# The planner of a fused HGRN2 attention and FFN kernel: DMA transfers planned as a queue, later loads for chunks 5 to 7

## The chip, the cores and the metric

The kernel runs on one core of one Trainium2 chip. The time of a run is the device time of that core in microseconds, and the time of a kernel is the median of its runs. The engines are named as in the profile: PE is the tensor engine's matmul, PEld its weight load, DVE the vector engine, ACT the scalar engine, POOL the general-purpose engine, SP the engine that issues nearly all DMA transfers here. Each engine executes its own instructions in the order in which they were written.

## The reference

Two stages follow each other. The first is a gated linear attention, the second a feed-forward network with a product in the place of an activation function.

```python
f = 1.0 / (1.0 + np.exp(-f_logit))            # B, H, S, D = 4, 8, 768, 48
for t in range(S):
    state = f[:, :, t, :, None] * state + np.einsum('bhd,bhe->bhde', k[:, :, t], v[:, :, t])
    y[:, :, t] = np.einsum('bhd,bhde->bhe', q[:, :, t], state)
x = y.transpose(0, 2, 1, 3).reshape(B * S, H * D)   # 3072 tokens x 384
out = (((x @ w1) * (x @ w2)) @ w3) @ w_out         # 384 -> 1024 -> 1024 -> 384
```

The inputs of the attention are float32. The four weights are float64, and the kernel reads their 64-bit words as pairs of 32-bit words.

## The kernel before, in words

**Tiling.** The 4 x 768 tokens are cut into 24 chunks of 128 tokens, called units u, six for each of the four sequences. The feed-forward network works on six blocks of 512 tokens, that is, four chunks each. A tile of q, k or f of one chunk has 112 partitions (two groups of 48 with a gap) and 512 columns.

**The attention of a chunk.** `front(u)` loads f, k and q (two DMA transfers of 96 KB each, L366 to L368) and v (one of 192 KB). ACT takes the sigmoid (`gates`, L380). DVE scans the products of the gates forward (L388) and backward (L410) and scales q (L404) and k (L418) with them. PE forms the pairs q times k (L431), transposes K (L455), and multiplies with v and with the state that is carried on. ACT copies the results out of PSUM: A (L562), kt (L589), the blocks of the state for the first chunks (`blocks`, L699), the last gate products (L393) and the outcome ys (L710). DVE updates the state (L689, L690). POOL masks A (L571). The first four chunks use one form of these steps and turn ys into xt on PE and ACT (`moved` L739, `settled` L744). The later chunks use half-size products, and write ys to DRAM (`written`, L731, two transfers) and read it back transposed as xt (`gathered`, L734, one transfer).

**The weights.** `fetch` (from L1103 on) loads a piece of a weight (L1138) into one of the landing places of the tile `place` and converts its words: ACT takes the magnitude (L1157) and the other word (L1160), DVE shifts (L1163, L1164), sets the sign (L1168) and joins (L1174). A landing place is free for a later piece once the pieces that used it before have passed DVE. There are twelve pieces of w1 and w2 (512 KB each), four of w_out (768 KB) and eight of w3 (1 MB). PE multiplies w3 with w_out once (`fold`, L1221), so that each token needs only the product with the folded matrix wc.

**The feed-forward network.** Block 0 forms `a` and `b` with plain products on PE (`part`; its products are issued by L761, as most products of this stage are), ACT keeps `a` (`keep_a`, L798) and DVE multiplies `b` into it (L803). Block 1 does this for half of its columns, for chunks 4 and 5 first and then for 6 and 7; the rest of block 1 and the later blocks use a scheme of seven products instead of eight (`seven`), with sums of xt made by DVE (L831). `down` multiplies with wc in the same way, and two stores (L1053) write each part of the output.

**What sets the order.** Nothing above is written in its final order. The class `Plan` gathers tasks, each with an engine, a cost in microseconds, its dependencies, a priority, and a `lag` that a task on another engine has to wait for after it. `order` is a list scheduler: again and again it takes, of all tasks whose dependencies are planned, the one that can start first (then by priority, then by number), and puts it at that time. At the end the tasks are emitted in the order of the planned starts, and this fixes the order of each engine's instructions. The planned times do not reach the chip: there an instruction waits for what it needs, and what stands behind it on its engine waits too. Before the first planned PE task, and where the plan has PE idle in the first 35 us (`FULL`), warm-up products (L268) are put in.

A transfer is planned by `moves` as a task of SP (0.45 us, the issue) and a task of an engine called DMA (bytes over a rate). At most eight transfers are under way, by the slot `lane`: an issue waits for the one eight places before it to have landed.

The lines that the change touches are those of `Plan.add`, `Plan.order`, `moves`, the loads and the costs in `front`, the calls of `moves` for yt and xt in `rest`, and the one for a weight piece in `fetch`.

Of the kernel before, what the change touches and what calls it, by code (L numbers as in the profile page):

```python
# [52 lines left out]
KM = DM // P  # L53
# [14 lines left out]
HIGH = float.fromhex("0x1.dffffep+16")  # L68
W = C // 2
FULL = 35.0  # L70
FLOOR = 2.0**-60
RANGE = 2.0**-40


class Plan:
# [13 lines left out]

        self.pools[name] = [None] * n  # L90

    def add(self, eng, cost, emit, deps=(), prio=0.0, takes=(), frees=(), lag=0.2, slack=0.0):


        t = {
            "eng": eng, "cost": cost, "emit": emit, "deps": [d for d in deps if d is not None], "prio": prio,
            "takes": list(takes), "frees": list(frees), "lag": lag, "slack": slack, "at": None, "end": None, "no": len(self.tasks),
        }
        self.tasks.append(t)
        return t  # L100

    def order(self):
        free, done, left = {}, [], list(self.tasks)
        enders = {}
        for t in self.tasks:
            for f in t["frees"]:
                enders.setdefault(id(f), []).append(t)

        def after(t, ds):

            if any(d["end"] is None for d in ds):
                return None
            return max([0.0] + [d["end"] + (d["lag"] + t["slack"] if d["eng"] != t["eng"] else 0.0) for d in ds])

        def places(t, name):

            ends = [(after(t, enders[id(h)]) if h else 0.0, i) for i, h in enumerate(self.pools[name])]
            return [e for e in ends if e[0] is not None]

        def start(t):  # L120

            waits, at = list(t["deps"]), free.get(t["eng"], 0.0)
            for name in t["takes"]:
                if name in self.pools:
                    ends = places(t, name)
                    if not ends:
                        return None
                    at = max(at, min(ends)[0])
                    continue
                n, taken = self.slots[name]  # L130
                if len(taken) >= n:
                    waits += enders[id(taken[-n])]
            ready = after(t, waits)
            return None if ready is None else max(at, ready)

        while left:
            at, _, _, t = min(
                ((at, t["prio"], t["no"], t) for t in left if (at := start(t)) is not None), key=lambda x: x[:3]
            )
            t["at"], t["end"] = at, at + t["cost"]  # L140
            free[t["eng"]] = t["end"]
            for name in t["takes"]:
                if name in self.pools:
                    t["got"] = min(places(t, name))[1]
                    self.pools[name][t["got"]] = t
                else:
                    self.slots[name][1].append(t)
            left.remove(t)
            done.append(t)
        return sorted(done, key=lambda t: (t["at"], t["no"]))  # L150
# [44 lines left out]
def ranged(ctx, tc, q, k, f_logit, v, w1, w2, w3, w_out, out, ident, w12, wc, left):  # L195
# [56 lines left out]
    plan = Plan()  # L252
# [73 lines left out]
    def past(u, n, *names):  # L326
        return [tk[u - n][nm] for nm in names if u >= n and nm in tk[u - n]]

    def moves(n, size, rate, emit, deps, prio, late=0.0):


        for j in range(n):
            i = plan.add("SP", 0.45, (lambda: None) if j else emit, [d] if j else deps, prio - j * 1e-3, takes=["lane"], lag=0.6)
            d = i
            t = plan.add("DMA", size / n / rate, lambda: None, [i], prio - j * 1e-3, lag=1.3 + late, frees=[i])
        return t

    def loaded(dst, u):
# [3 lines left out]
    def front(u):  # L342

        s, t = st[u], tk[u]
        n0 = need(u)

        def load(dst, src):
            def emit():
                if dst is fs[0] and u == 0:

                    nc.sync.dma_start(dst[0:64], src[u].rearrange("two d n -> (two d) n")[0:64])
                    nc.sync.dma_start(dst[rows(1)], src[u, 1])
                    return
                for par in range(2):
                    nc.sync.dma_start(dst[rows(par)], src[u, par])
            return emit

        fu, qu, ku = (x[u if u < 4 else u % n] for x, n in ((fs, 2), (qs, 3), (ks, 2)))

        def free(n, *names):  # L360

            if u < 4:
                return []
            return asked[8:9] + [tk[u - n if u - n >= 4 else u % n][nm] for nm in names]

        t["lf"] = moves(2, 197, 250, load(fu, f_logit), free(2, "g"), n0 - 30)  # L366
        t["lk"] = moves(2, 197, 250, load(ku, k), free(2, "k"), n0 - 29.5)
        t["lq"] = moves(2, 197, 250, load(qu, q), free(3, "q"), n0 - 29)  # L368

        def load_v():  # L370
            s["v"] = at(12288 + NQ, DM) if u == 3 else loads.tile([P, DM], F32, name="vt")
            loaded(s["v"], u)

        t["lv"] = moves(
            1, 197, 320, load_v, [] if u == 3 else past(u, 4 if u in (4, 5, 6) else 3, "v", "s"),
            n0 - (28.2, 28.2, 28.2, 29.6, 12)[min(u, NPE)],
        )

        def gates():
            nc.scalar.activation(gate[u % 2][:, 0:NQ], fu, AF.Sigmoid)  # L380

        t["g"] = plan.add("ACT", 0.65, gates, [t["lf"]] + past(u, 2, "r") + past(u, 3, "G"), n0)
        if u % NCH and "G" in tk[u - 1]:
            tk[u - 1]["G"]["deps"].append(t["g"])

        def forward():
            s["P"] = one.tile([R, NQ], F32, name="fwd")
            nc.vector.tensor_tensor_scan(s["P"], gate[u % 2][:, 0:NQ], floor, 0.0, ALU.mult, ALU.max)  # L388

        t["p"] = plan.add("DVE", 1.25, forward, [t["g"]] + past(u, 1, "q", "i", "l"), n0)  # L390

        def last():
            nc.scalar.copy(lasts[:, u], heads(s["P"])[:, :, C - 1])  # L393

        t["l"] = plan.add("ACT", 0.2, last, [t["p"]], n0)

        def ends():
            nc.vector.reciprocal(heads(back)[:, :, C - 1], heads(s["P"])[:, :, C - 1])

        t["i"] = plan.add("DVE", 0.18, ends, [t["p"]] + past(u, 1, "r"), n0)  # L400

        def scale_q():
            s["Q"] = work3.tile([R, NQ], F32, name="Q")
            nc.vector.tensor_tensor(s["Q"], qu, s["P"], ALU.mult)  # L404

        t["q"] = plan.add("DVE", 0.7, scale_q, [t["p"], t["lq"]] + past(u, 3, "v", "a"), n0 + 0.1)

        def backward():
            s["R"] = one.tile([R, NQ], F32, name="bwd")
            nc.vector.tensor_tensor_scan(  # L410
                s["R"][:, ::-1], gate[u % 2][:, NQ:0:-1], back[:, ::-1], 0.0, ALU.mult, ALU.max
            )

        t["r"] = plan.add("DVE", 1.25, backward, [t["i"]] + past(u, 1, "k"), n0)

        def scale_k():
            s["K"] = work.tile([R, NQ], F32, name="K")
            nc.vector.tensor_tensor(s["K"], ku, s["R"], ALU.mult)  # L418

        t["k"] = plan.add("DVE", 0.7, scale_k, [t["r"], t["lk"]] + past(u, 2, "a", "t"), n0)  # L420
        if u in (2, 3):
            t["k"]["frees"].append(coming)

# [206 lines left out]
    def rest(u):  # L630
        s, t = st[u], tk[u]
        opens, closes = u % NCH == 0, u % NCH == NCH - 1
        n0 = need(u)
        if u < NPE:
# [6 lines left out]
                takes=["f"],  # L641
# [76 lines left out]
        n = u // UB  # L718
# [27 lines left out]
        before = blk[n - 2]["up"] if n >= 2 else []  # L746
        if u < NPE:
            t["z"] = plan.add("PE", 1.6, moved, [t["y"]], n0 - 996, takes=["f"], frees=[moving])
            t["x"] = plan.add("ACT", 0.55, settled, [t["z"]] + before, n0 - 20, frees=[t["z"]])
        else:  # L750
            t["z"] = moves(2, 197, 250, written, [t["y"]], n0 - 100)
            t["x"] = moves(1, 197, 250, gathered, [t["z"]] + before, n0 - 100)


    blk = [{} for _ in range(NB)]
# [353 lines left out]
    def fetch(loads_, a, prio, subs, deps=()):  # L1109
# [5 lines left out]
        total = subs[-1][1]  # L1115
        if not wide:
# [7 lines left out]
            waits = [d for sub in subs for d in sub[4]]  # L1124
            ld = plan.add("SP", 1.9 * total / 512, plain, waits, prio, lag=2.0)
            return [ld] * len(subs)
        load_no = len(users)
# [6 lines left out]
        held = holders(where, 2 * total)  # L1134

        def load():
            for place_, src in loads_:
                nc.sync.dma_start(raw.rearrange("p (a m) -> p a m", a=a)[place_], src.bitcast(U32))  # L1138

        ld = moves(1, total, 380, load, held, prio, max(0.0, 3.5 - 1.2 * load_no) if load_no < 4 * KM else 3.0)  # L1140
        asked.append(ld)
        got = []
        users.append((where, 2 * total, got))
# [179 lines left out]
    for t in plan.order():  # L1323
        if t["eng"] == "PE" and t["at"] < FULL:
            n = int((t["at"] - ready_at) / 0.43)
# [343 lines left out]
```

## Time and profile before

| | us |
|---|---|
| median of 3 runs | 477.67 (477.29 to 477.99) |
| profiled execution, its own time | 482.72 |
| profiled execution, span of the core | 481.0 |
| PE busy | 468.7 |
| PEld busy | 400.4 |
| DVE busy | 362.8 |
| ACT busy | 141.1 |
| POOL busy | 62.5 |

The mean granted clock of PE is 0.995 of full speed. The profiled execution took 5.05 us more than the median of the runs. Busy times of different engines overlap; the largest of them does not say alone what a change in one stage is worth. An instruction's line of the profile gives its start, its length, what it writes and reads, and in brackets how long its engine had been idle and what ended that. A transfer goes from its issue on SP to its landing.

### The profile page before, as it was taken

To read this page: it belongs to the slowest core of one execution; us is meant where nothing else is said; L and a number is where in the kernel's file an instruction comes from. 1 tells how busy PE (TensorE), PEld (TensorE's weight loads), DVE (VectorE), ACT (ScalarE), POOL (GpSimd) and SP (SyncE) were. 2 spreads that over 40 slices of the span, in tenths; PEclk is the share of its full clock that TensorE was granted. 3 is DMA by queue.
4 is the path that set the end of the run, shared out by engine and by line. 5 is a ranking of instruction groups with operands and counts; after the bars stand their busy time and mean duration, and the time that the engine had idled before them with its cause. 6 is when DMAs were issued, how large, how long until landed. Compare 5 with 4: busy or idle time off the path is not lost.

```text
span 481.0 us, 11341 instructions
## 1 busy us (share of the span) xinstructions
PE 468.7 (97%) x4667; PEld 400.4 (83%) x4667; DVE 362.8 (75%) x706; ACT 141.1 (29%) x310; POOL 62.5 (13%) x88
## 2 busy tenths in 40 slices
PE   8899999999999899999999999999999999999996
PEld 7788644656799688889988889988899888889995
DVE  7999699999999689899999567357653667664541
ACT  4697456462313334432432110001100110110000
POOL 9300000013303133312422100000000000000000
PEclk9999999999999899999999999999999999999999
DMA  6899277743415566446531002000111000000011
GB/s 183 269 387 236 54 278 246 260 138 100 134 50 162 163 172 169 115 132 169 148 110 46 18 18 65 34 33 2 34 33 58 9 0 1 0 1 1 34 66 37
DMA packets 36618, 50.10 MB, mean 104 GB/s; under 512 B 4546, under 2 KB 26050, under 8 KB 35538
## 3 DMA queue, kind: packets, MB, share of 16 engines
q1 hardware_dynamic: 36562, 49.33, 33.6%
q8 instruction: 37, 0.61, 0.6%
q14 instruction: 19, 0.16, 0.1%
HBM read 40.67 MB, written 8.65 MB: 103 GB/s over the span
## 4 chain that ended last, share of the span: by engine, by line
PE 73%; DVE 13%; DMA 6%; POOL 3%; issue 2%; ACT 1%; SPq 1%; DVEq 0%; POOLq 0%; ACTq 0%
PE f L761 62%; DVE place L1168 2%; PE f L1221 2%; DMA place<-in_w_dram 2%; PE py L515 2%; DVE place L1174 2%; DMA place<-in_w_out_dram 2%; PE f L455 2%; PE pa L441 2%; PE pa L548 2%; PE py L534 1%; DMA f<-in_f_logit_dram 1%; SPq L1138 1%; POOL ab L306 1%; DVE place L1253 1%
## 5 line engine op out<-in xcount | busy, mean ns | idle before, releaser
L761 PE MATMUL f<-xt,w 128*128 128x256 f32 (+1 forms) x600 | 162.8, 401 | 3.2 <-ACT gate L380 2.0
L761 PEld LDWEIGHTS f<-xt,w 128*128 128x128 f32 x600 | 114.1, 192 | 29.5 <-issue 10.0
L761 PE MATMUL f<-place 128*128 128x192 f32 (+1 forms) x504 | 112.1, 349 | 0.1
L761 PEld LDWEIGHTS f<-place 128*128 128x128 f32 x504 | 87.7, 190 | 6.2 <-DVE place L1010 0.4
L571 POOL TENSOR_SCALAR_AFFINE_SELECT A<-A 64x512 f32<-64x512 f32 (+1 forms) x44 | 40.7, 925 | 120.3 <-ACT A L565 110.5
L1221 PE MATMUL f<-place 128*128 128x384 f32 x128 | 42.8, 489 | 0.2 <-DVE place L1174 0.2
L864 ACT COPY a<-f 128x256 f32<-128x256 f32 x36 | 13.4, 373 | 93.2 <-PE f L761 78.0
L1221 PEld LDWEIGHTS f<-place 128*128 128x128 f32 x128 | 23.8, 190 | 16.5 <-DVE place L1174 0.8
L761 PE MATMUL f<-xt,place 128*128 128x256 f32 x144 | 37.3, 382 | 0.0
L761 PE MATMUL f<-wc,ab 128*128 128x192 f32 x192 | 35.2, 327 | 0.0
L761 PEld LDWEIGHTS f<-wc,ab 128*128 128x128 f32 x192 | 32.0, 190 | 0.5
L410 DVE TENSOR_TENSOR_SCAN bwd<-gate,back 112x512 f32<-112x512 f32 x24 | 30.0, 1249 | 0.8
L388 DVE TENSOR_TENSOR_SCAN fwd<-gate,floor 112x512 f32<-112x512 f32 x24 | 29.6, 1233 | 1.1 <-ACT gate L380 0.3
L761 PEld LDWEIGHTS f<-xt,place 128*128 128x128 f32 x144 | 26.6, 189 | 3.3
L888 DVE TENSOR_TENSOR place<-f,a 128x256 f32<-128x256 f32 x36 | 15.3, 424 | 18.6 <-PE f L761 18.4
L1157 ACT ACTIVATE place<-place 128x512 f32<-128x512 f32 (+2 forms) x24 | 21.3, 886 | 8.2 <-DVE w L1174 3.8
L1160 ACT ACTIVATE place<-place 128x512 f32<-128x512 uint32 (+2 forms) x24 | 21.1, 885 | 5.1 <-DMA place<-in_w_out_dram 5.1
L674 POOL TENSOR_TENSOR G<-lasts,gate 112x4 f32<-112x4 f32 x20 | 11.1, 556 | 87.3 <-ACT lasts L393 55.2
L710 ACT ACTIVATE ys<-py 112x512 f32<-112x512 f32 x20 | 11.9, 596 | 35.6 <-PE py L534 34.6
L761 PE MATMUL f<-place,w 128*128 128x256 f32 x72 | 21.4, 379 | 0.0
L899 DVE TENSOR_TENSOR ab<-f,place 128x256 f32<-128x256 f32 x36 | 15.2, 423 | 6.2 <-PE f L761 5.3
L997 DVE TENSOR_TENSOR place<-ab 128x512 f32<-128x512 f32 x24 | 16.9, 702 | 3.5 <-PE f L761 3.5
(126 smaller groups left out, 642.9 us busy)
## 6 DMA issues: line engine op xcount, KB each, us to landing
place<-in_w_dram SPq DMA_DIRECT2D x8, 1024.0 KB, 4.7
place<-in_w_dram SPq DMA_DIRECT2D x12, 512.0 KB, 9.7
out_dram<-o SPq DMA_DIRECT2D x24, 192.0 KB, 1.9
q<-in_q_dram SPq DMA_DIRECT2D x46, 96.0 KB, 2.8
vt<-in_v_dram SPq DMA_DIRECT2D x23, 192.0 KB, 3.4
k<-in_k_dram SPq DMA_DIRECT2D x44, 96.0 KB, 2.3
f<-in_f_logit_dram SPq DMA_DIRECT2D x43, 96.0 KB, 2.5
yt<-ys SPq DMA_DIRECT2D x40, 96.0 KB, 2.4
```

The lines of the kernel that those rows point to most:

```text
L388: nc.vector.tensor_tensor_scan(s["P"], gate[u % 2][:, 0:NQ], floor, 0.0, ALU.mult, ALU.max)
L410: nc.vector.tensor_tensor_scan(s["R"][:, ::-1], gate[u % 2][:, NQ:0:-1], back[:, ::-1], 0.0, ALU.mult, ALU.max)
L571: nc.gpsimd.affine_select(out=a, in_=a, pattern=pattern, compare_op=ALU.is_ge, fill=0.0, base=0, channel_multiplier=-1,)
L710: nc.scalar.activation(ys, py, AF.Copy, accum_out=ysum[:, u : u + 1])
L761: nc.tensor.matmul(out_, lhsT=lhs[i], rhs=rhs[i], start=start and i == 0, stop=i == len(lhs) - 1, skip_group_check=True,)
L864: nc.scalar.copy(q["a"], q["X"])
L888: nc.vector.tensor_tensor(ups["u3", k], q["Y"], q["a"], ALU.add)
L899: nc.vector.tensor_tensor(m if which else to(tok, half), q[bank_], m, ALU.add)
L997: nc.vector.tensor_tensor(abs_[j], x, y, op)
L1157: nc.scalar.activation(m, hi.bitcast(F32), AF.Abs)
L1160: nc.scalar.activation(lo.bitcast(F32), lo, AF.Copy, bias=2.0, scale=2.0**-51)
L1221: nc.tensor.matmul(w3s["p", jc], lhsT=w3s[jc][:, kc * P : kc * P + P], rhs=wos[:, kc], start=(kc == 0), stop=(kc == KF - 1),)
```

## The change

The planner's picture of the DMA transfers and of the early part is changed; no instruction of the computation is added or taken away.

- Every engine's planned time begins at 0.6 (`BEGIN`) instead of 0.
- Of several DMA tasks that could start first, the one asked for first is taken (`rank`), where before the priority decided.
- In two windows of planned time (`CROWDED`) a transfer's cost is multiplied by 1.6 or 1.3.
- Rates for f, k, q and yt go from 250 to 300, for weights from 380 to 400. The lag after an issue goes from 0.6 to 0.85, after a transfer from 1.3 to 1.1. The extra lag of a weight piece, which was 3.5 falling by 1.2 for each of the first pieces, then 0, and 3.0 for those of w_out and w3, becomes 0.5 for all.
- `scale_k` is planned at 1.3 for chunks 1 to 3, and at 0.72 for others, instead of 0.7; `scale_q` at 0.72.
- A task may have a time `since` before which it isn't planned. f, k and q of chunks 5 to 7 get one: 22 us (`AHEAD`) before the time at which the chunk is due.

```diff
+BEGIN = 0.6
+SURE = 0.5
+SURE_X = 0.0
+SURE_W = 2.0
+CROWDED = [(13.5, 19.5, 1.6), (33.0, 46.0, 1.3)]
+AHEAD = 22.0
...
     def order(self):
-        free, done, left = {}, [], list(self.tasks)
+        free, done, left = dict.fromkeys(("PE", "DVE", "ACT", "POOL", "SP"), BEGIN), [], list(self.tasks)
...
-            waits, at = list(t["deps"]), free.get(t["eng"], 0.0)
+            waits, at = list(t["deps"]), max(free.get(t["eng"], 0.0), t["since"])
...
+        def rank(t):
+            return t["deps"][0]["end"] - 1e6 if t["eng"] == "DMA" else t["prio"]
+        def slower(t, at):
+            return max([1.0] + [by for a, b, by in CROWDED if a <= at < b]) if t["eng"] == "DMA" else 1.0
...
-                ((at, t["prio"], t["no"], t) for t in left if (at := start(t)) is not None), key=lambda x: x[:3]
+                ((at, rank(t), t["no"], t) for t in left if (at := start(t)) is not None), key=lambda x: x[:3]
             )
-            t["at"], t["end"] = at, at + t["cost"]
+            t["at"], t["end"] = at, at + t["cost"] * slower(t, at)
...
-    def moves(n, size, rate, emit, deps, prio, late=0.0):
+    def moves(n, size, rate, emit, deps, prio, late=0.0, since=0.0):
...
-            i = plan.add("SP", 0.45, (lambda: None) if j else emit, [d] if j else deps, prio - j * 1e-3, takes=["lane"], lag=0.6)
+            i = plan.add("SP", 0.45, (lambda: None) if j else emit, [d] if j else deps, prio - j * 1e-3, takes=["lane"], lag=0.85, since=since)
             d = i
-            t = plan.add("DMA", size / n / rate, lambda: None, [i], prio - j * 1e-3, lag=1.3 + late, frees=[i])
+            t = plan.add("DMA", size / n / rate, lambda: None, [i], prio - j * 1e-3, lag=1.1 + late, frees=[i])
...
-        t["lf"] = moves(2, 197, 250, load(fu, f_logit), free(2, "g"), n0 - 30)
-        t["lk"] = moves(2, 197, 250, load(ku, k), free(2, "k"), n0 - 29.5)
-        t["lq"] = moves(2, 197, 250, load(qu, q), free(3, "q"), n0 - 29)
+        since = n0 - AHEAD if 4 < u < 8 else 0.0
+        t["lf"] = moves(2, 197, 300, load(fu, f_logit), free(2, "g"), n0 - 30, since=since)
+        t["lk"] = moves(2, 197, 300, load(ku, k), free(2, "k"), n0 - 29.5, since=since)
+        t["lq"] = moves(2, 197, 300, load(qu, q), free(3, "q"), n0 - 29, since=since)
...
-        t["q"] = plan.add("DVE", 0.7, scale_q, [t["p"], t["lq"]] + past(u, 3, "v", "a"), n0 + 0.1)
+        t["q"] = plan.add("DVE", 0.72, scale_q, [t["p"], t["lq"]] + past(u, 3, "v", "a"), n0 + 0.1)
...
-        t["k"] = plan.add("DVE", 0.7, scale_k, [t["r"], t["lk"]] + past(u, 2, "a", "t"), n0)
+        t["k"] = plan.add("DVE", 1.3 if 0 < u < 4 else 0.72, scale_k, [t["r"], t["lk"]] + past(u, 2, "a", "t"), n0)
...
-            t["z"] = moves(2, 197, 250, written, [t["y"]], n0 - 100)
-            t["x"] = moves(1, 197, 250, gathered, [t["z"]] + before, n0 - 100)
+            t["z"] = moves(2, 197, 300, written, [t["y"]], n0 - 100)
+            t["x"] = moves(1, 197, 250, gathered, [t["z"]] + before, n0 - 100, SURE_X)
...
-        ld = moves(1, total, 380, load, held, prio, max(0.0, 3.5 - 1.2 * load_no) if load_no < 4 * KM else 3.0)
+        ld = moves(1, total, 400, load, held, prio, SURE)
```

What the new plan does to the order of each engine's instructions, so far as the prediction speaks of it:

- SP: its first 40 transfers keep their order. After them q of chunk 4 and the first two pieces of w_out now stand ahead of f, k and q of chunk 5; f, k and q of chunks 6 and 7 stand behind the later pieces of w_out and the first of w3. Around 150 us the store of yt of chunk 7 stands ahead of v of chunk 10, and f of chunk 14 behind the xt load of chunk 7.
- ACT: the first weight piece's two steps (L1157, L1160) stand ahead of `blocks` of chunk 1, kt and A of chunk 2 and the last gate products of chunk 3. The gate of chunk 4 stands ahead of a `keep_a`, and that of chunk 5 behind a later weight step.
- DVE: scaling of k and q of chunk 2 come before the state of chunk 1; the forward scan of chunk 4 is moved behind the joining of the first piece of w3.
- PE: the attention steps of chunks 0 to 3 are interleaved differently; in block 1 the up products of two of the column groups (jc4 and jc5) on chunks 4 and 5 come about 30 us later, and products of `seven` earlier. There are 9+5 warm-up products, where there were 9+4.

More of the change, by code (lines that the diff above doesn't have):

```diff
@@ L90, in pool, with add @@
         self.pools[name] = [None] * n
-    def add(self, eng, cost, emit, deps=(), prio=0.0, takes=(), frees=(), lag=0.2, slack=0.0):
+    def add(self, eng, cost, emit, deps=(), prio=0.0, takes=(), frees=(), lag=0.2, slack=0.0, since=0.0):
         t = {
             "eng": eng, "cost": cost, "emit": emit, "deps": [d for d in deps if d is not None], "prio": prio,
-            "takes": list(takes), "frees": list(frees), "lag": lag, "slack": slack, "at": None, "end": None, "no": len(self.tasks),
+            "takes": list(takes), "frees": list(frees), "lag": lag, "slack": slack, "since": since, "at": None, "end": None, "no": len(self.tasks),
         }
```

## The prediction

> **What bounds the kernel now.** I read the engine totals and the chain of the page first.
>
> ```profile
> PE 468.7 (97%) x4667; PEld 400.4 (83%) x4667; DVE 362.8 (75%) x706; ACT 141.1 (29%) x310; POOL 62.5 (13%) x88
> PE 73%; DVE 13%; DMA 6%; POOL 3%; issue 2%; ACT 1%; SPq 1%; DVEq 0%; POOLq 0%; ACTq 0%
> ```
>
> TensorE fills 97% of the span and 73% of the chain that ended last. The change adds no arithmetic, so only places where PE stands still or runs slowly can pay. A table by stage (window, length; busy us and count of PE, PEld, DVE, ACT, POOL; granted clock; DMA share; GB/s) finds them:
>
> ```profile
> 36.00:48.00 12.00, 12.00 (x57) 10.55 (x57) 10.98 (x23) 8.53 (x17) 0.00 (x0) 1.00 0.97 237
> 48.00:52.00 4.00, 2.80 (x14) 2.15 (x13) 0.38 (x2) 1.55 (x3) 0.00 (x0) 1.00 0.13 42
> 52.00:75.00 23.00, 23.00 (x67) 12.36 (x66) 22.52 (x39) 10.75 (x17) 0.71 (x2) 1.00 0.62 202
> 83.00:126.00 43.00, 42.98 (x428) 27.00 (x429) 42.02 (x55) 20.24 (x33) 7.11 (x8) 1.00 0.51 164
> 158.00:166.00 8.00, 6.04 (x42) 4.47 (x44) 3.65 (x10) 1.98 (x6) 1.40 (x2) 0.79 0.66 183
> 166.00:285.00 119.00, 118.91 (x2232) 105.91 (x2222) 102.14 (x211) 39.85 (x105) 29.83 (x38) 1.00 0.41 112
> ```
>
> Two rows have room: 48 to 52, where DVE works 0.38 of 4 us, and 158 to 166, where PE loses time twice, to idling and to a clock of 0.79. From 166 to 285 only 0.09 us is free. The waits name the causes (total, times, longest):
>
> ```profile
> ACT place L1160 <- DMA place<-in_w_out_dram: 5.1, 1, 5.1
> DVE ab L803 <- ACT ab L798: 3.7, 1, 3.7
> DVE place L831 <- DMA xt<-yt: 2.6, 1, 2.6
> ```
>
> The first two are one stop: ACT, whose instructions run in their written order, holds L1160 for the second piece of w_out; behind it stands keep_a (L798), and DVE stands behind that. The chain says why that piece is late (start, length):
>
> ```profile
> 40.74 0.33 DVE place L1163
> 41.06 9.30 DMA place<-in_w_out_dram
> 50.37 0.02 issue
> ```
>
> It was issued when DVE set its landing place free, behind f and k of chunk 5, and took 9.30 us; the third piece, issued at 58.19, landed at 62.56 (4.37 us). The second stop in the timelines of PE and of SP, the issuing engine:
>
> ```profile
> 157.75 1.47 PE L761 MATMUL f<-xt,w 128*128 128x256 f32 x6
> 161.19 4.51 PE L761 MATMUL f<-xt,w 128*128 128x256 f32 x12 [1.96 <-ACT gate L380]
> ```
>
> ```profile
> 150.28 1.72 SPq L340 DMA_DIRECT2D vt<-in_v_dram  x1
> 152.10 0.86 SPq L731 DMA_DIRECT2D yt<-ys  x2
> ...
> 155.40 0.88 SPq L355 DMA_DIRECT2D f<-in_f_logit_dram  x2
> 156.37 0.39 SPq L734 DMA_DIRECT2D xt<-yt  x1
> ```
>
> PE is put down to ACT's gate, but the xt of chunk 7, issued 156.37, landed at 161.10 and both PE and DVE (L831) start then. Its y was ready at 149.88 (end of L710), yet the store of it went out at 152.10 behind v of chunk 10. Finally ACT early on:
>
> ```profile
> 18.83 0.71 ACT L699 COPY sb<-S 48x192 f32<-48x192 f32 x2 [1.44 <-DVE S L690]
> ...
> 19.94 0.54 ACT L589 COPY kt<-py 128x448 f32<-128x448 f32 x1
> 20.76 0.20 ACT L393 COPY lasts<-fwd 112x4 f32<-112x4 f32 x1 [0.28 <-DVE fwd L388]
> 20.87 1.00 ACT L562 COPY A<-pa 128x1024 f32<-128x1024 f32 x1
> 21.98 0.69 ACT L1157 ACTIVATE place<-place 128x512 f32<-128x512 f32 x1
> ```
>
> The first weight piece lands at 21.96 and ACT takes it at once, having filled the time before with attention work.
>
> [...] 2.34 us of idling was followed by 3.41 us at 0.5. [...] the yt stores here took 2.29 to 2.84.
>
> **The change part by part.** The same instructions run, apart from one more warm-up matmul (9+5 for 9+4), which lies in an early wait. What differs is their order. I take the profiled execution: span 481.0, whole time 482.72, which is 5.05 above the median of 477.67.
>
> (1) *ACT from 18 to 26.* The first piece's L1157 and L1160 now stand ahead of blocks of chunk 1 (L699, 0.71), last of 3 (L393, 0.20), kt of 2 (L589, 0.54) and A of 2 (L562, 1.00): 2.45 us of work, and DVE, PE and POOL wait for it. From the starts shown: L1157 at 21.98, L1160 ends its slot at 23.15, L699 to 23.86, L710 with its sum (0.58 + 0.20) to 24.6, L393 to 24.8, the next L1157 to 25.4, kt to 25.95. PE's v·k (0.67) ends at 26.7 and DVE's state of chunk 2, at 24.95 before, starts at 26.75: DVE is 1.8 us late. It has no spare time from there to 47.92 (10.98 of 12 us busy), so the delay reaches 47.92, where it falls into the 3.70 us of idling. Cost: nothing, up to 3.7 us of delay; without that cover, 1.8. PE stands perhaps 2 to 4 us in pieces around 21 to 26. Its own largest gap there before is 1.24. A half-clock window over short matmuls would cost up to 1.7 us (half of 3.41), inside the same cover in part.
>
> (2) *w_out piece 2.* f and k of chunk 5 (4 x 96 KB) are moved behind it. If only their bytes go, 393 KB at 237 GB/s (36 to 48) is 1.7 us: landing at 48.7. If the issue follows DVE's late L1163, 41.06 + 1.8 = 42.9, plus 4.37 like piece 3, plus 0.8 for q of chunk 4 (196 KB) beside it: 48.1. I take 48.4. keep_a then starts 0.86 (50.37 to 51.23, with one L1160) plus 0.6 (gate of chunk 4 is now ahead of it) later: 49.9, DVE at 50.3 instead of 51.62. Both of DVE's bounds (49.7 from its delay, 50.3 from ACT) lie under 51.62, so PE and DVE resume **1.3 us earlier**; range 0.3 to 1.9. f5 and q5 land later, but gate of 5 is also moved behind later weight work on ACT. DVE is busy 22.52 of 23 us to 75 and PE 42.98 of 43 to 126, so the gain is carried, less a little for the scan of chunk 4 (1.23), which now follows w3 work: I take **-1.2**.
>
> (3) *SP from 150 to 157.* The yt store moves ahead of v of chunk 10, f of chunk 14 behind the xt load. Store at about 149.4 to 150.3; then v (0.5 to 1.7), two out stores (1.28) and q (0.87) remain: xt goes out at 152.9 to 153.8 instead of 156.37. At the median latency of its 20 transfers, 2.9, it lands at 155.8 to 156.7; at the 4.73 seen here, up to 158.5. PE needs it earlier than before: the first up product of jc4 on chunks 4 and 5 (L761 x6 at 157.75, 1.3 us to the next), which stood ahead of it, is moved some 30 us on. So 158.95 becomes 158.95 - 1.3 - 1.2 = 156.4. The stop is 0 to 2.1 us; I take 0.7 and no slow window, since 1.20 us at 50.4 brought none. Before it cost 2.3 idle + 0.21 x 8 = 1.7 of clock, 4.0. Result: **-3.3**.
>
> (4) *166 to 285.* First products of the second block come earlier, the two moved ups later. All are PE work that keeps its length. PE had 0.09 us free, so nothing can be gained; a new wait could cost. I take 0, range 0 to +4 (a second stop with its slow window).
>
> (5) f6, f7, k6, q6, q7 behind w_out and w3 pieces: hidden by the 30 us or more until their gates run after 85; if not, their PE work is delayed at most until DVE's queue comes round, within (4).
>
> Sum: -1.2 - 3.3 = -4.5, 482.72 to 478.2, and 477.67 to **473.2** at the median. The stop of (3) hangs on one 4.73 us latency and the executions without a profile may not all have had it: this is the weak term.
>
> **Rivals.** A, *only the early gain*: the xt stop is absent or short without the profile, or comes again (4.73 us latency at the later end). For it: its transfers' median is 2.9. Against it: the queue position alone would be late at 2.9 as well, 156.37 + 2.9 = 159.3 against 158.95. It gives 477.67 - 1.2 = 476.5. B, *nothing*: w_out piece 2 lands no sooner as its issue waits for DVE, and the old stop keeps its size: 477.7. C, *slower, through ACT at 18 to 22*: the wait for the first piece has PE's attention chain and DVE behind it. Should DVE's delay pass 3.7 us the cover is gone and each further us counts. That needs the first piece 2 us later, or twice the 2.45 us of work to be awaited in turn by PE and DVE; with 4.2 of delay and PE at half clock (1.7), +0.5 +1.7 = +2.2: 479.9. For it: DVE has no other slack up to 48. Against it: 1.8 is half of the cover.
>
> **How the numbers follow.** Forecast (both gains) 0.42, A 0.25, B 0.10, C or a new stop of (4) 0.23. 0.2% of the time, 0.96 us, is about what a measurement tells from no change. So faster 0.67, same 0.10, slower 0.23. The likeliest case alone spans 471.5 (no stop left, DVE 1.9 early) to 475.5 (1.0 more of each). The range reaches from 471.5 to 480.0, past C's 479.9; what is left out is a full second stop with its slow window.
>
> **What would show it.** Right: ACT idle of some 4 us at an L1157 before 22; w_out piece 2 landed by 49; DVE's idling before L803 at most 2 us and PE back by 50.5; xt of chunk 7 issued before 154; no granted clock under 1 from 150 to 285. Wrong: a PE gap over 2 us with a slow window in the reordered stretch, a slow window at 21 to 28, or DVE still stopped until 51.6 at an L803.

## The result and the profile after

The changed kernel takes 481.96 us (median of 8 runs, 477.28 to 483.15), the kernel before 477.83 beside it (477.29 to 479.47). The ratio is 1.0062 with a 95% interval of 1.0037 to 1.0087: **slower**, where 473.2 and faster had been forecast. This ratio, like those of the table below, is estimated from all the runs together and is not the quotient of the two medians, which is 1.0086. The profiled execution of the changed kernel took 481.71 us, its span is 480.0. That of the kernel before had 482.72 and 481.0. The two profiles thus show a gain of 1.0 us, and the medians a loss of 4.1 us (the ratio, 3.0 us). The profiled execution of before was no usual one, and this is half of the story: of 162 later runs of that kernel, on five chips, one took 482.90 us, and all others 480.70 or less.

All line numbers of the changed kernel are 14 or 15 higher than before. Engine totals and chain of the page of the changed kernel:

```profile
PE 468.1 (98%) x4669; PEld 399.9 (83%) x4669; DVE 361.8 (75%) x706; ACT 142.3 (30%) x310; POOL 61.3 (13%) x88
PE 73%; DVE 12%; DMA 7%; POOL 3%; issue 3%; ACT 1%; SPq 0%; DVEq 0%; POOLq 0%; ACTq 0%
```

The work is the same. The table by stage of the changed kernel, with the columns of the table in the prediction:

```profile
36.00:48.00 12.00, 12.00 (x57) 10.55 (x57) 11.69 (x25) 9.43 (x17) 0.00 (x0) 1.00 0.82 222
48.00:52.00 4.00, 4.00 (x20) 3.51 (x19) 3.06 (x8) 1.83 (x5) 0.20 (x1) 1.00 0.00 0
52.00:75.00 23.00, 23.00 (x63) 11.78 (x62) 21.41 (x34) 11.67 (x17) 0.00 (x0) 1.00 0.73 241
83.00:126.00 43.00, 43.00 (x474) 27.27 (x476) 42.03 (x55) 19.04 (x33) 6.99 (x8) 1.00 0.53 169
158.00:166.00 8.00, 7.01 (x103) 5.82 (x106) 3.73 (x10) 1.03 (x3) 0.03 (x1) 0.79 0.45 128
166.00:285.00 119.00, 119.00 (x2174) 105.95 (x2165) 100.34 (x210) 40.57 (x105) 29.22 (x38) 1.00 0.40 113
```

From 48 to 52 DVE works 3.06 us instead of 0.38: the stop for the second w_out piece is mostly gone. But from 158 to 166 the mean clock is 0.79, exactly as before: for 3.41 of these 8 us it is at 0.5. Such a stretch is called half clock below. The waits of the changed kernel for transfers:

```profile
ACT place L1172 <- DMA place<-in_w_dram: 5.9, 2, 3.1
PE f L776 <- DMA xt<-yt: 2.2, 1, 2.2
ACT place L1175 <- DMA place<-in_w_out_dram: 1.9, 1, 1.9
DVE ab L818 <- ACT ab L813: 0.8, 1, 0.8
```

The w_out wait fell from 5.1 to 1.9 and DVE's behind it from 3.7 to 0.8. In their place ACT now waits 5.9 us for weights at L1172, and PE still waits 2.2 us for the xt of chunk 7. The timelines of PE and SP around that second stop, changed kernel:

```profile
155.36 1.47 PE L776 MATMUL f<-xt,w 128*128 128x256 f32 x6
158.99 5.83 PE L776 MATMUL f<-xt,w 128*128 128x256 f32 x18 [2.15 <-DMA xt<-yt]
```

```profile
150.18 0.86 SPq L746 DMA_DIRECT2D yt<-ys  x2
151.13 0.41 SPq L354 DMA_DIRECT2D vt<-in_v_dram  x1
...
153.56 0.39 SPq L749 DMA_DIRECT2D xt<-yt  x1
```

The load was issued at 153.56, 2.8 us earlier than before, and landed at 158.94: it took 5.39 us. And the early part on ACT:

```profile
17.34 0.48 ACT L759 COPY xt<-f 128x384 f32<-128x384 f32 x1 [0.33 <-PE f L754]
20.88 0.68 ACT L1172 ACTIVATE place<-place 128x512 f32<-128x512 f32 x1 [3.06 <-DMA place<-in_w_dram]
...
22.01 0.70 ACT L714 COPY sb<-S 48x192 f32<-48x192 f32 x2
22.73 0.60 ACT L725 ACTIVATE ys<-f 112x512 f32<-112x512 f32 x1
```

ACT stands for 3.06 us on the first weight piece, with `blocks` and `outcome` of chunk 1 behind it: DVE had the state that `blocks` reads ready at 19.82, and `blocks` started at 22.01. PE stops for 1.83 us because of it:

```profile
23.60 1.60 PE L754 MATMUL f<-ys,ab 112*128 112x128 f32 x12 [1.83 <-ACT ys L725]
```

In this execution no half clock follows, and the first up product (the first product of the feed-forward network) starts at 34.73, as early as before.

### The profile page after: what moved, and what is told of

It reads as the page before. It is cut to its first block, busy times and chain, and to the rows that moved or that the text cites. A ratio compares the mean times of both kernels' runs of the same rounds, so it can differ in the third digit from the quotient of the medians.

```text
span 480.0 us, 11366 instructions
## 1 busy us (share of the span) xinstructions
PE 468.1 (98%) x4669; PEld 399.9 (83%) x4669; DVE 361.8 (75%) x706; ACT 142.3 (30%) x310; POOL 61.3 (13%) x88
## 4 chain that ended last, share of the span: by engine, by line
PE 73%; DVE 12%; DMA 7%; POOL 3%; issue 3%; ACT 1%; SPq 0%; DVEq 0%; POOLq 0%; ACTq 0%
PE f L776 61%; PE f L1236 4%; DMA place<-in_w_dram 3%; DMA place<-in_w_out_dram 3%; PE py L530 2%; PE pa L456 1%; PE pa L563 1%; PE py L549 1%; DVE w L1183 1%; DVE place L1189 1%; PE f L470 1%; DMA xt<-yt 1%; DVE place L1178 1%; POOL ab L320 1%; DVE place L1268 1%
## 5 line engine op out<-in xcount | busy, mean ns | idle before, releaser
L1172 ACT ACTIVATE place<-place 128x512 f32<-128x512 f32 (+2 forms) x24 | 21.2, 887 | 15.2 <-DMA place<-in_w_dram 5.9
L914 DVE TENSOR_TENSOR place<-f,place 128x256 f32<-128x256 f32 x36 | 15.3, 424 | 4.5 <-PE f L776 2.9
```

The costliest lines, as they stand in the source:

```text
L914: nc.vector.tensor_tensor(m if which else to(tok, half), q[bank_], m, ALU.add)
L1172: nc.scalar.activation(m, hi.bitcast(F32), AF.Abs)
```

## The experiments

After the result two theories stood against each other. **X**: PE's stop before the xt of chunk 7, with its half clock, is rare in the kernel before and regular in the changed one. **E**: the hold of ACT on the first weight piece costs early time. Each run below is set against the kernel before on its own chip.

| run | median us | ratio to before | 95% interval |
|---|---|---|---|
| the changed kernel, result above | 481.96 | 1.0062 | 1.0037 to 1.0087 |
| before, again | 478.56 | 1.0012 | 1.0000 to 1.0025 |
| changed, again | 483.46 | 1.0124 | 1.0093 to 1.0155 |
| fill: jc4 products back ahead of the xt | 480.37 | 1.0051 | 1.0023 to 1.0078 |
| away: before, jc4 and jc5 products moved off | 480.42 | 1.0067 | 1.0028 to 1.0106 |
| first: ACT's first weight steps back | 479.96 | 1.0040 | 1.0022 to 1.0057 |
| fill_first: both back | 476.67 | 0.9976 | 0.9965 to 0.9988 |
| piece_ahead: before, ACT's steps moved up | 479.67 | 1.0034 | 1.0015 to 1.0052 |
| warmed: changed, PE kept busy at 22 us | 479.86 | 1.0044 | 1.0028 to 1.0061 |
| soon: fill_first without the later loads | 477.46 | 0.9981 | 0.9961 to 1.0001 |
| shifted: first, PE's stream 61 products longer | 481.09 | 1.0067 | 1.0047 to 1.0087 |
| half_shifted: first, 31 products longer | 479.60 | 1.0019 | 0.9995 to 1.0043 |
| held: first, five loads behind the xt later | 477.79 | 0.9996 | 0.9974 to 1.0017 |

The second row is the same program as its comparison: 0.1% is not resolved here.

### Both kernels again

No edit.

> The kernel before, unchanged, for more executions with spans, clocks and a second trace. Theory X (the stop of PE before xt of chunk 7 and the half clock behind it, 4.0 us together, are in few executions of before and in nearly all of after): the trace shows no stop over 1.5 us at 158 to 161, clock 1.00 to 285, span about 476 to 477. Theory E (the difference is made early, at 22 to 24 us): the stop is there again at 2.3 us, span about 481, as in the first profile.

> The changed kernel, unchanged. Theory X: in its trace PE stops again over 2 us before xt of chunk 7 lands, at 157 to 159, followed by 3.41 us at half clock, span about 480. Theory E: a half-clock window at 23 to 28 us beside the PE stop at 22 to 23.6, in addition to or without the one at 159. Median about 482 in both.

In the second trace of before PE's stop at 158 is short:

```profile
159.01 2.83 PE L761 MATMUL f<-xt,w 128*128 128x256 f32 x12 [1.24 <-ACT gate L380]
```

The clock stays at 1.00 to the end of PE's work and the span is 476.9. The xt load was there too, issued 154.96 and 3.96 us on its way. DVE's product after the second w_out piece starts at 50.17, not at 51.62. So both rooms that the prediction meant to win were smaller in this execution than in the first profile. The changed kernel's second trace, ACT and then PE:

```profile
21.65 0.66 ACT L1172 ACTIVATE place<-place 128x512 f32<-128x512 f32 x1 [3.66 <-DMA place<-in_w_dram]
...
23.48 0.60 ACT L725 ACTIVATE ys<-f 112x512 f32<-112x512 f32 x1
```

```profile
21.34 0.60 PE L470 MATMUL py<-ident,K 112*128 112x112 f32 x4
24.35 2.49 PE L754 MATMUL f<-ys,ab 112*128 112x128 f32 x12 [2.41 <-ACT ys L725]
...
37.01 1.25 PE L776 MATMUL f<-xt,w 128*128 128x256 f32 x5
```

PE waits 2.41 us for the ys that stands behind ACT's weight steps, then runs at half clock (12 products in 2.49 us where 1.60 was taken in the first trace of this kernel) and starts the first up product at 37.01. In both traces of before, and in the first one of the changed kernel, that is at 34.73 or 34.74. At 160.44 comes the second stop (2.10 us, clock at 0.5 after it). The two traces can be laid side by side: the last of the eight folds starts 1.82 us later than in before's second trace (121.11 against 119.29), the end of PE's work is 4.53 us later (476.87 against 472.34). So in this pair of executions 1.8 us come from the early part, 2.7 us from after it. Both theories have a share. A mean granted clock of 0.996 or less, which a half-clock window of 3.41 us in 481 us gives (0.5 x 3.41 / 481 = 0.0035), stood in 7 of the 8 runs of the changed kernel (480.49 to 483.15 us; the eighth, at 1.0, took 477.28) and in all 4 of the repeat. Of the 162 runs of before 7 have such a mean. (PE's clock also falls after its last product: in before's first trace that product ends at 476.21, and the clock is 0.5 from 479.36. This took at most 0.003 of a mean in the traces, as in those of shifted and piece_ahead, with means of 0.997 and a clock of 1.00 up to 470 us.) Six of these seven took only 478.07 to 478.41 us, among the usual runs. Their half clock cost little, wherever it was; the seventh is the run of 482.90. So the dear stop of the first profile is rarer in before than half clocks are.

### Put the jc4 products back, or move them off alone

```diff
 # fill, in the changed kernel, after the up products of block 1 are planned
+for i in (8, 10, 12, 14):            # those on chunks 6 and 7
+    s["up"][i]["deps"].append(s["up"][5])      # follow both of jc4 on chunks 4 and 5
 # away, in the kernel before
+for i in (4, 6):                     # jc4 and jc5 on chunks 4 and 5
+    s["up"][i]["deps"].append(s["up"][11])     # follow jc1 on chunks 6 and 7
```

> The changed kernel with the two up products of jc4 on chunks 4 and 5 (2.6 us of PE work) put back ahead of the first product that needs xt of chunk 7; the orders before 156 us are untouched, some later ones shift. Theory X: the stop shrinks from 2.15 to under 0.5 us, no half clock at 159, median 477.5 to 478.5, that is 3.5 to 4.5 under the changed kernel. Theory E (loss at 22 to 24): median stays at 481 to 482.

> The kernel before with only this: the up products of jc4 and jc5 on chunks 4 and 5 come after the first four products that need xt of chunk 7, as in the changed kernel; nothing before 155 us is moved. Theory X: PE stops for 2.5 to 3.5 us before xt of chunk 7 in nearly every execution, half clock behind it, median 481 to 483. Theory E: median stays at 477.8, or the stop is no more frequent than before.

In fill the stop at 158 is gone, as X said: PE's products run through, although the xt load took 5.12 us. But the median fell only to 480.37. Its trace shows why, in the table by stage and in PE's timeline:

```profile
25.00:33.00 8.00, 8.00 (x70) 6.99 (x71) 5.75 (x11) 5.26 (x10) 2.52 (x2) 0.57 1.03 402
158.00:166.00 8.00, 8.00 (x168) 6.99 (x161) 7.62 (x15) 3.24 (x9) 2.11 (x2) 1.00 0.73 214
```

```profile
24.04 1.83 PE L754 MATMUL f<-ys,ab 112*128 112x128 f32 x12 [2.18 <-ACT ys L725]
...
38.27 2.11 PE L776 MATMUL f<-xt,w 128*128 128x256 f32 x9
```

The half clock now lasts some 7 us at 25 to 33 and the first up product waits until 38.27. The early loss is there without the late one.

Away missed its expectation in the trace: its xt load took only 3.01 us, the stop was 0.73 us, and no half clock followed. The end of PE's work is 1.64 us later than in before's second trace, but 1.78 us of that stood already at the last fold (121.07), which the edit doesn't reach: there the second w_out piece was late again (DVE's product at 51.94). So removing the filler, the two jc4 products that PE had to do while the load was under way, is not shown to make the stop by itself; the slow load belongs to it. Away's runs are nevertheless slower than before's (1.0067). Two of the five had a mean clock of 0.996, the other three 0.999 or 1.0, so a half clock doesn't account for most of them. Why they are slower stays open.

### Put ACT's steps back, or move them up alone

```diff
 # first: in the changed kernel's final order; fill_first: the same on top of fill
-for t in plan.order():
+e0, b0 = parts[0][0]["deps"][:2]      # rest and magnitude of weight piece 1
+b1 = parts[1][0]["deps"][1]           # magnitude of piece 2
+tasks = [t for t in plan.order() if not any(t is x for x in (e0, b0, b1))]
+to = [t is tk[2]["m"] for t in tasks].index(True) + 1      # behind A of chunk 2
+tasks[to:to] = [b0, e0, b1]
+for t in tasks:
 # piece_ahead: in the kernel before, the same with b0 and e0 alone
+to = [t is tk[1]["b"] for t in tasks].index(True)          # ahead of blocks of chunk 1
+tasks[to:to] = [b0, e0]
```

> The changed kernel with ACT's first three steps on weight pieces 1 and 2 put back behind the attention work of chunks 1 to 3 (blocks, outcome, last, kt, A); every other engine's order and all later ACT work as in the changed kernel. Theory E (ACT standing on the first weight piece stops PE at 22 to 24.6 us, and the half clock behind it delays the first up product from 34.7 to 37 us): no PE gap over 1 us before 30, clock 1.00 there, first up product by 34.8, median 1.5 to 3 us under the changed kernel, so 479.5 to 482, with the stop before xt of chunk 7 still there. Rival (only the stop at 158 counts): median within 0.7 us of the changed kernel.

> The kernel before with one thing: ACT's two steps on the first weight piece moved ahead of blocks of chunk 1, kt and A of chunk 2 and last of chunk 3, as the change does. Theory E: PE stands over 2 us at 20 to 25, in most executions with half clock behind it, first up product at 36.5 to 38.5 instead of 34.73, median 479 to 481. Rival (the delay is covered by DVE's idling before the second w_out piece): median within 0.7 us of before.

> Both put back: the ACT steps as in the run before this one and the two up products of jc4 ahead of the first product that needs xt of chunk 7. If the two causes E and X are all of the loss, the median is 475.5 to 477.3, at or below the kernel before (477.6 to 477.8), clock 1.00 from start to 470. If a third cause is in the reordered stretch from 166 to 285 us, it stays above 478.5.

In first the early stop is gone and the late one stays, at 1.57 us and with no half clock behind it:

```profile
21.68 1.52 PE L754 MATMUL f<-ys,ab 112*128 112x128 f32 x12
...
34.37 1.89 PE L776 MATMUL f<-xt,w 128*128 128x256 f32 x8
...
158.92 4.15 PE L776 MATMUL f<-xt,w 128*128 128x256 f32 x18 [1.57 <-DMA xt<-yt]
```

The first up product starts at 34.37, and against before the ratio falls from 1.0124 or 1.0062 to 1.0040 (its interval overlaps that of the second value, not that of the first). PE does have one gap over 1 us, 1.32 up to 28.91, behind POOL. In other runs of first a half clock did come: 7 of the 17 had a mean clock of 0.996 or less.

Piece_ahead gives the loss from the other side: 1.0034 on the kernel before by this one edit. The trace shows the hold of ACT:

```profile
20.66 0.68 ACT L1157 ACTIVATE place<-place 128x512 f32<-128x512 f32 x1 [3.06 <-DMA place<-in_w_dram]
21.24 0.67 ACT L1160 ACTIVATE place<-place 128x512 f32<-128x512 uint32 x1
21.81 0.70 ACT L699 COPY sb<-S 48x192 f32<-48x192 f32 x2
```

It is milder than what was expected: PE's gaps stay under 0.7 us and the first up product starts at 35.13. The first weight piece landed early here, at 20.64, where it came at 21.96 and 21.85 in the traces of before, and PE's order at this place is not that of the changed kernel. This execution took 477.49 us, one of the fast ones. A mean clock of 0.996 or less stood in 9 of the 16 runs, against 4 of the 49 of before on the same chip; where in those runs it fell is not known.

With both put back the kernel is faster than before: 0.9976 (0.9965 to 0.9988). Two rows of its table by stage:

```profile
150.00:166.00 16.00, 16.00 (x318) 14.14 (x318) 15.11 (x29) 6.93 (x19) 5.07 (x7) 1.00 0.73 207
166.00:285.00 119.00, 119.00 (x2119) 105.90 (x2118) 100.52 (x212) 37.88 (x99) 25.36 (x35) 1.00 0.38 108
```

PE has no gap from 150 to 285. None of its 20 runs had a mean clock under 0.998. So the two causes, ACT's hold at 18 to 22 us and the uncovered wait for the xt of chunk 7, are all of the loss, and no third one lies in the reordered stretch. Set against before's second trace, this one has its last fold 0.63 us earlier (118.66 against 119.29) and the end of PE's work 1.77 us earlier (470.57 against 472.34). The rest of 1.14 us is about the stop of 1.24 us which before has at 158 and this kernel doesn't. One trace of each kernel stands behind this account of the gain.

### The half clock or the late work

```diff
 # in the changed kernel, when the tasks are emitted
+if t is tk[1]["z"]:     # moved of chunk 1, where PE stops at 22 us
+    idle(5)
```

> The changed kernel with five warm-up products (about 1.9 us of PE) put in front of the step at which PE stops at 22 us; nothing else moved. If the half clock behind the stop is what makes it dear: no clock under 1 before 150, first up product near 34.7, median 1.5 to 3 us under the changed kernel. If the late attention work by itself is what costs: first up product stays at 36.5 or later and the median within 0.7 us of the changed kernel.

```profile
21.96 2.34 PE L282 MATMUL f<-floor 112*128 112x256 f32 x10
24.59 1.60 PE L754 MATMUL f<-ys,ab 112*128 112x128 f32 x12 [0.29 <-ACT ys L725]
...
35.72 1.46 PE L776 MATMUL f<-xt,w 128*128 128x256 f32 x6
```

The clock stays at 1.00 to the end of PE's work, and none of the five runs had a mean under 0.997. The first up product lies at 35.72, between 34.7 and 37. By this trace and the changed kernel's second one, some 1.0 us is the late work itself, and the other 1.3 us the half clock. The changed kernel's first trace, with a stop of 1.83 us and no half clock, lost nothing up to 34.73; so the half clock is the dear part, and the share of the late work is not settled. The median, 479.86, is in the range that was expected for this case, but the ratio's interval (1.0028 to 1.0061) overlaps that of the changed kernel beside the result. PE stands 1.92 us for the xt of chunk 7 in this trace too, again without a half clock.

### The later loads alone

```diff
 # on top of fill_first
-AHEAD = 22.0
+AHEAD = 220.0     # no later time for f, k and q of chunks 5 to 7
```

> The kernel of both repairs (ACT's first weight steps behind the attention work, the two jc4 products ahead of the xt of chunk 7), with the later loads taken back: f, k and q of chunks 5 to 7 have no time before which they may not be planned, so f and k of chunk 5 are again ahead of the second piece of w_out. PE's order is untouched. If the later loads are what brought PE back earlier at 49 to 50 us: w_out piece 2 lands 0.7 to 2 us later, DVE's product after the stop starts at 50.2 to 51 instead of 49.4, median 0.5 to 1.3 us over the run with both repairs (476.67), so 477.2 to 478. If not: within 0.3 us of 476.67.

The second w_out piece lands at 49.01 instead of 47.61 (it now has f and k of chunk 5 ahead of it), and DVE's product starts at 50.29 instead of 49.40. But two products further the difference is 0.18 us (54.43 against 54.25), the last fold starts 0.32 later and the span ends 0.13 later. The ratios, 0.9981 and 0.9976, can't be told apart. In these two executions the later loads do what they should to the piece and bring next to nothing at the end.

### Why the xt load is slow

```diff
 # shifted, on top of first: ahead of all PE work
-idle(9)
+70 products of 16 x 16
 # half_shifted, on top of first
-idle(9)
+33 products of 16 x 16, then idle(7)
 # held, on top of first: SP's order
-xt of chunk 7; k of 12, v of 11, q of 13; yt of chunk 8
+xt of chunk 7; yt of chunk 8; k of 12, v of 11, q of 13
```

> The changed kernel with ACT's first weight steps put back, and 70 small products (16 x 16) in place of the first nine warm-up products, so that PE's instruction stream is 122 instructions longer ahead of everything else: PE's 16 KB instruction fetches then fall at other places of the work, some 3 us away from where they were. If the fetch beside it is what makes the xt load of chunk 7 take 4.8 to 5.8 us: no fetch between its issue and its landing, 2.3 to 3.5 us to landing, PE's stop there under 0.5 us, median about 478 instead of 479.96. If the load is slow for another reason: 4.5 us or more again, stop 1.5 to 2.2 us, median near 480.

> The changed kernel with ACT's first weight steps put back, and 33 small products (16 x 16) ahead of seven of the nine first warm-up products: PE's stream is 31 products longer, 124 instruction records, about half of the distance between two of its 16 KB fetches (the run with 70 products had moved it by 244, nearly a whole distance, so the fetch fell beside the xt load again). If that fetch is what makes the xt load of chunk 7 take 4.6 to 5.8 us: the fetch is now 3 us or more away from the load, which takes 2.3 to 3.5 us, PE stands under 0.5 us before it, median 1 to 2 us under the run with the ACT steps alone (479.96). If it isn't: 4.5 us or more to landing and a stop of 1.5 to 2.2 us again.

> The changed kernel with ACT's first weight steps put back, and SP's five loads that follow the xt load of chunk 7 (k of 12, v of 11, q of 13) issued only behind the next yt store, so that nothing is asked for in the 2 us behind the xt load. If the loads behind it make the xt load slow: 2.3 to 3.5 us to landing instead of 4.76, PE's stop before it under 0.5 us, median 1 to 2 us under the run with the ACT steps alone (479.96). If something else does (PE's 16 KB instruction fetch, which again begins 1 to 2 us after the issue, or the transfers ahead): 4.5 us or more to landing, stop 1.5 us or more, median near 480.

The transfers of the changed kernel from 155 to 159, one column for 0.1 us, moved like this:

```profile
GB/s 282 215 236 266 476 282 277 292 297 328 312 266 277 231 220 169 251 215 184 333 210 369 246 225 179 154 164 56 56 20 41 15 15 51 205 287 246 123 205 138
```

From 157.7 to 158.4, half a microsecond before the xt lands, hardly anything moves (15 to 56 GB/s). A 16 KB instruction fetch on another queue had begun at 155.5 and took 1.92 us; there are 37 of them in this trace, one for about 250 of PE's products and weight loads. That was the reason for looking at the fetch. Neither shift moved it away: it began 2.0 us after the xt was issued in shifted, and 1.2 us after it in half_shifted (in first 2.0). The load took 4.64 and 4.89 us. Shifted also lost early, since PE's first real products ran slower there (the first four took 0.98 us, 0.57 in the changed kernel; the next sixteen 2.08 and 1.16). Both are inconclusive on the fetch. The traces with before's order of SP say more. There such a fetch also begins 1.0 to 2.0 us after the xt was issued, and two of these four loads took 2.82 us (piece_ahead) and 3.01 us (away). A fetch beside the load is thus not enough to make it slow.

Held answers its question in its trace:

```profile
157.37 4.15 PE L776 MATMUL f<-xt,w 128*128 128x256 f32 x18 [1.61 <-DMA xt<-yt]
```

With nothing issued behind it for 1.4 us the load still took 4.51 us and PE stood 1.61 us, so in this execution the loads behind it are not the cause. Its twelve runs fit the other case: the median is 477.79, the ratio 0.9996 has an interval (0.9974 to 1.0017) that ends below that of first (1.0022 to 1.0057), and none of them had a mean clock under 0.998. In the trace the gain against first is all early (DVE's product after the w_out piece at 49.21 against 50.84, the last fold at 118.51 against 120.13), where the edit doesn't reach; whether the edit helps in the other runs stays open. What makes this one load take 4.5 to 5.8 us in every trace with the changed order of SP stays open; in before's order it took 2.8 to 4.7.

## Why the prediction was wrong

The chance for slower was 0.23, and of its mechanism, rival C, the place was right: ACT at 18 to 22 us. Of the six signs that were named for a right forecast, the first trace of the change shows four as named, and a fifth nearly (ACT idle for 3.06 us, where some 4 were named); only the half clock at 159 spoke against it. What the range left out by name, "a full second stop with its slow window", is what came. The likeliest case failed at these steps.

**(1) ACT from 18 to 26.** The chain of delays was right: `blocks`, kt and A of chunk 2 behind the weight steps, DVE's state of chunk 2 at 25.93 in the first trace of the change (26.75 forecast), PE standing at 22. The step that failed is "Cost: nothing, up to 3.7 us of delay". It set the half clock at 1.7 us, in part inside the cover. In the first trace the stop was 1.83 us, without half clock, and cost nothing. With stops of 2.18 and 2.41 us the half clock came: the first up product then moved by 2.3 to 3.5 us. The cover, DVE's idling before the second w_out piece, was not always 3.7 us but 2.26 us in before's second trace. By the warm-up run the half clock is more than half of the early loss in the second trace.

**(2) w_out piece 2.** It landed at 47.16 (48.4 forecast), and DVE's product came at 48.97 (50.3 forecast): 2.65 us earlier than in before's first trace, where 1.3 had been expected. The step that failed is "so the gain is carried". At 68.58 ACT waited 2.84 us for the first w3 piece, DVE 1.12 us behind it, and the last fold started 1.14 us earlier than in before's first trace. That this is near the -1.2 of the sum is luck: twice the gain was made, and over half of it lost again. Against before's second trace the same fold is 0.32 us late. The run without the later loads shows the same: 0.9 us at 49 is 0.13 us at the end.

**(3) SP from 150 to 157.** Issue at 153.56 (152.9 to 153.8 forecast): right. Need of PE at 156.8 (156.4): right. The term of the sum that was mis-sized is the latency: 2.9 was taken, with 4.73 as the upper end, and it was 5.39 (5.80 in the second trace). The stop was 2.15 us and not 0.7, and "no slow window" was wrong: the 1.20 us at 50.4, which had brought none, said nothing about a stop of 2 us. The part from the last fold to the end of PE's work took 355.81 us, 0.35 more than in before's first trace, where 3.3 less had been forecast. The jc4 product had been the cover of this load, and the working counted its removal only as an earlier need. With it back the same slow load costs nothing (fill).

**(3) again, the base.** The 4.0 us to be won were those of one execution (3.7 by PE's own line, which shows 1.96 us of idling; the 2.3 in the sum is the wait of the weight loads). The text called this the weak term, and named that the profile lay 5.05 us above the median, but still put the whole 3.3 into a sum that was then moved to the median. One of 162 later runs of before was as slow as that profile, so this gain didn't exist for the median. What the change did was to make the rare stop regular.

**(4) and (5).** Right: PE is busy for 119.00 of 119.00 us from 166 to 285, and no later load shows.

On the clock, the prediction had two stops of before's first trace to go by: 1.20 us, followed by no half clock, and 2.34 us, followed by 3.41 us at 0.5. By PE's own count the second is 1.96 us; 2.34 is the same stop by its weight loads. After PE's start, in which the warm-up products were first 0.43 us apart and then 0.22 (from 8.3 us in before's first trace, from 5.4 us in that of the changed kernel), no stop up to 1.92 us was followed by a half clock in the traces here, and every one from 1.96 us was, until PE's last product. The half clock lasted 3.41 us, or about twice that (6.8 us in fill). The 2.29 to 2.84 us that the prediction gives for the yt stores are those of chunk 7; all 34 yt stores whose landing before's first trace shows took 1.95 to 3.97 us.

## What to carry to other kernels

Before a gain is booked, ask whether the stop in the profile is in most executions: a profile well above the median of the runs may hold a rare stop. The mean clock of each run (here 0.996 or less) tells how many had a half clock, and only its time whether that one was dear. A planner that takes an engine's wait as free will put it in front of work that others wait for; an instruction that may be held for a transfer belongs behind the short steps that feed PE (ahead of them it cost 0.34% in piece_ahead). And independent work ahead of a load's first use should be measured against the spread of that load's latency, not its median: here the two jc4 products, put back, let a load of 5.12 us pass without a stop.

## What was not expected of the hardware

- In these traces stops of PE that differ little in length differ in what came after them: 1.57, 1.61, 1.64, 1.78, 1.83 and 1.92 us passed at a clock of 1.00, and 1.96, 2.10, 2.15, 2.18 and 2.41 us were followed by 3.41 us or about 7 us at 0.5. The changed kernel, whose two traces have stops of 1.83 to 2.41 us, took 477.28 us in the run with a mean clock of 1.0, and 480.49 to 483.15 us in those with 0.990 to 0.996.
- Two loads of the same size and form differ by more than a factor of two: the 192 KB xt loads of the changed kernel took 2.31 to 5.39 us in one execution.
